# Twelve weight loads of a sparse-attention-and-FFN kernel, each issued as two transfers of 64 partitions

## The chip, the cores and the metric

The kernel runs on one core of a Trainium2 chip. The metric is device time in microseconds (us), measured from the start of the program's launch on the chip to its end; three runs of the kernel before gave 817.62, 818.4 and 819.12 us, median 818.4. Traces come from one profiled execution, with times counted from the start of its span.

## The reference

Attention with two sparse masks, then a feed-forward network with a gate. There are 8 batches, 8 heads, 576 positions and 64 elements per head; the network takes the 4608 tokens from 512 to 2048 and back to 512.

```
scores = matmul(q, k.T) / sqrt(64)
mask   = (0 <= rel < 32)                         for heads 0..3
         (rel >= 0) & (pos_k % 32 == pos_q % 32) for heads 4..7
attn   = softmax(where(mask, scores, -1e9))
x      = (attn @ v), heads side by side          # [4608, 512]
h      = x @ w_in                                # [4608, 2048]
g      = h if h >= 1; 0 if h <= -1; (h + 1)**2 / 4 between
out    = g @ w_out                               # [4608, 512]
```

## The kernel before, in words

The weights come in 8-byte numbers. The host part lays them out as `w[f, p, 1024]`: 16 units `f` of 128 columns of `w_in` (part `i = 0`, 512 numbers in each partition) and the 128 rows of `w_out` that belong to them (part `i = 1`). `load_w(f, i)` (L312 to L320) brings one part of one unit, 128 partitions of 4 KB, 512 KB in all, with one `dma_start` on SyncE's queue (SP, L319). Every part is then turned into two 4-byte tiles, a high and a low one, by five operations: A (ACT, L343), L (ACT, L347), B (DVE, L351), C (POOL, L355) on the raw words, then D (ACT or DVE, L364), which writes the high tile, and E (DVE, L368), which writes the low one. The matmuls of unit `f` (`up`, h, L775, and `down`, o, L820) read those tiles. `load_piece` (L322) loads the last two units in another way and isn't touched.

The first 3 chunks of 512 tokens go through `up`, the gate and `down` unit by unit; the other 3072 tokens go in three blocks through a form with seven products in place of eight (L917, L1005), whose factors are written to DRAM and fetched again. The attention of a batch is worked in four groups of scores: two of local heads (operands `qk_l`) and two of strided heads (`qk_s`); scores are L482, the turned probabilities go through PE's transposes, and for the later batches partly through DRAM (`spread`, L643, and `gather`, L654, which writes 32 partitions of the tile pT with each transfer).

All loads stand in one queue, SP, in the order of the code: at the start the four score operands of batch 0, then

```
load_w(0, 0, loaded[0, 1, "qk"][0:1, 0, 0:1])
load_v(0, 0); load_v(0, 1)
load_w(1, 0)
load_v(0, 2); load_v(0, 3)
load_w(2, 0)
stage(4)            # raw_0.1, raw_1.1, raw_2.1, raw_3.0, raw_3.1
for p in range(2): load_qk(1, p)
stage(6)            # raw_4.0, raw_4.1, raw_5.0, raw_5.1
```

(raw_3.1 stands for part 1 of unit 3, and so on; the lines are L1044 to L1055). The first load waits for an ACT copy (L318) that reads the score operands. The framework gives every transfer one of eight lanes in turn (DMAHW0 to DMAHW7 in the rows below), and an issue on a lane waits until the transfer before it on that lane, the eighth before, has landed. The order of the arithmetic is written out by hand in tables (BEGIN for the start, CONV for the conversions), so no scheduler moves it.

Of the kernel before, what the change touches and what calls it, by code (L numbers as in the profile page):

```python
# [17 lines left out]
P = 128  # L18
# [155 lines left out]
def tile_sparse_attention_then_ffn(  # L174
# [14 lines left out]
    nc = tc.nc  # L189
# [112 lines left out]
    wt, raws, pieces, held = {}, {}, {}, set()  # L302
    PLACES = (6, 7, 8, 9, 10, 11, 12, 13, 14, 15, 12, 13, 14, 15)
    w_v = w.bitcast(U32).rearrange("f p (i e t) -> f p i e t", i=2, t=2)
# [4 lines left out]
    def place(u, shape, dtype, name):  # L309
        return slot(f"w{u}", shape, dtype, name)  # L310

    def load_w(f, i, after=None):  # L312
        at = PLACES[f]
        if i == 0:
            held.add(at)
            raws[f] = place(at, [P, 2, DM, 2], U32, f"raw_{f}")
        if after is not None:
            nc.scalar.copy(raws[f][0:1, i, 0:1, 0].bitcast(F32), after)  # L318
        nc.sync.dma_start(raws[f][:, i], w_v[f][:, i])  # L319
        pieces[f, i] = [(raws[f][:, i], slice(0, DM))]  # L320

    def load_piece(f, i, k=0, pool=qk_p, tag="qk", of=1):  # L322
# [51 lines left out]
    def stage(n=len(PLACES)):  # L374
        nonlocal staged
        while staged < n and ((staged, 0) in pieces or PLACES[staged] not in held):
            if (staged, 0) not in pieces:
                load_w(staged, 0)
            load_w(staged, 1)
            staged += 1  # L380
# [662 lines left out]
    with tc.manual_schedule():  # L1043
        for p in range(4):  # L1044
            load_qk(0, p)
        load_w(0, 0, loaded[0, 1, "qk"][0:1, 0, 0:1])
        load_v(0, 0)
        load_v(0, 1)
# [127 lines left out]
```

## Time and profile before

| | |
|---|---|
| median of three runs | 818.4 us |
| the profiled execution: span | 815.5 us |
| the profiled execution: its own time beside the span | some 2.9 us around it, if it is a median run |
| PE busy | 806.2 us, 99% of the span |
| DVE, ACT, POOL busy | 574.7, 495.4, 232.5 us |
| bytes moved | 195.10 MB, mean 239 GB/s |
| granted TensorE clock | full in all 40 slices |

PE is TensorE, DVE VectorE, ACT ScalarE, POOL GpSimd, SP SyncE. PE is the engine that sets the time of most of the span; the DMA engines are at full share only in the first 40 us or so and at some places later. The profiled execution's own time wasn't recorded apart from the three runs; the 2.9 us are the median less the span.

### The profile page before, as it was taken

How to read it: one execution, taken by the hardware profiler on the slowest of the kernel's cores; microseconds unless marked ns; L12 is line 12 of the kernel's file. 1: busy time of each engine (PE TensorE's matmuls, PEld its weight loads, DVE VectorE, ACT ScalarE, POOL GpSimd, SP SyncE). 2: the span in 40 equal slices, each digit the busy share in tenths (PEclk: the TensorE clock that was granted, in tenths of full speed). 3: DMA queues.
4: the chain of work that ended last, by engine and by line, in shares of the span. 5: the costliest groups of instructions: out<-in, count | busy, mean ns of one | idle time of the engine just before them, and what ended most of it. 6: DMA issues, size and time to landing. Idle time of an engine off the chain costs nothing.

```text
span 815.5 us, 17861 instructions
## 1 busy us (share of the span) xinstructions
PE 806.2 (99%) x6969; PEld 656.9 (81%) x6969; DVE 574.7 (70%) x850; ACT 495.4 (61%) x866; POOL 232.5 (29%) x226
## 2 busy tenths in 40 slices
PE   8999999999999999999999999999999999999998
PEld 6788888878878888887878888888888888888886
DVE  5898868767548477776778876675589834558664
ACT  5888955545355365776775453778654647775442
POOL 5353544873347543023222000220120001114100
PEclk9999999999999999999999999999999999999999
DMA  9936437788868867987998768887666776666765
GB/s 344 408 138 201 153 111 274 265 298 278 265 221 299 286 243 257 304 287 247 285 288 266 216 203 249 263 265 228 193 193 213 232 235 196 196 192 190 216 200 170
DMA packets 101796, 195.10 MB, mean 239 GB/s; under 512 B 17105, under 2 KB 32465, under 8 KB 99665
## 3 DMA queue, kind: packets, MB, share of 16 engines
q1 hardware_dynamic: 92496, 164.60, 63.3%
q10 hardware_dynamic: 9216, 29.36, 9.4%
q8 instruction: 55, 0.90, 0.5%
q14 instruction: 29, 0.23, 0.1%
HBM read 147.26 MB, written 46.66 MB: 238 GB/s over the span
## 4 chain that ended last, share of the span: by engine, by line
PE 91%; DMA 5%; issue 1%; DVE 1%; ACT 1%; POOL 0%; SPq 0%; ACTq 0%; POOLq 0%
PE o L820 16%; PE h L775 16%; PE yo L1005 15%; PE y L917 15%; PE zo L1005 8%; PE z L917 7%; PE xo L1005 4%; PE x L917 4%; PE xp L669 3%; PE sc L482 3%; DMA wr<-kq 1%; DMA qk<-in_qk_s 1%; DMA there<-t 1%; DMA pT<-there 1%; DMA qk<-in_qk_l 1%
## 5 line engine op out<-in xcount | busy, mean ns | idle before, releaser
L917 PE MATMUL y<-x,wr 128*128 128x512 f32 x576 | 141.3, 392 | 0.0
L775 PE MATMUL h<-xq,w 128*128 128x512 f32 x576 | 140.0, 392 | 0.1
L1005 PE MATMUL yo<-hl,wr 128*128 128x512 f32 x576 | 132.8, 390 | 0.6 <-DMA wr<-kq 0.6
L820 PE MATMUL o<-gh,w 128*128 128x512 f32 x384 | 130.1, 399 | 0.0
L1005 PEld LDWEIGHTS yo<-hl,wr 128*128 128x128 f32 x576 | 108.0, 188 | 23.4 <-DMA wr<-kq 1.0
L775 PEld LDWEIGHTS h<-xq,w 128*128 128x128 f32 x576 | 107.4, 188 | 23.4 <-DVE xq L739 0.7
L917 PEld LDWEIGHTS y<-x,wr 128*128 128x128 f32 x576 | 107.4, 188 | 22.7
L820 PEld LDWEIGHTS o<-gh,w 128*128 128x128 f32 x384 | 72.1, 188 | 16.2
L820 PE MATMUL o<-gl,w 128*128 128x512 f32 x192 | 75.0, 391 | 0.0
L917 PE MATMUL z<-x,wr 128*128 128x512 f32 x288 | 73.7, 391 | 0.0
L957 POOL TENSOR_TENSOR ga<-gb,ga 128x1024 f32<-128x1024 f32 x9 | 21.6, 2397 | 167.5 <-DVE ga L785 141.7
L1005 PE MATMUL zo<-hl,wr 128*128 128x512 f32 x288 | 66.1, 390 | 0.0
L572 POOL TENSOR_TENSOR pr<-pr,st 128x384 f32<-128x384 f32 (+3 forms) x21 | 26.3, 1253 | 135.7 <-DVE st L595 64.5
L1005 PEld LDWEIGHTS zo<-hl,wr 128*128 128x128 f32 x288 | 54.0, 188 | 11.3
L917 PEld LDWEIGHTS z<-x,wr 128*128 128x128 f32 x288 | 53.8, 188 | 11.3
L782 ACT ACTIVATE tmp<-tmp 128x512 f32<-128x512 f32 x96 | 60.7, 632 | 3.0
L871 DVE TENSOR_TENSOR hl<-ga,hl 128x1024 fp32r<-128x1024 f32 x36 | 47.3, 1315 | 19.9 <-ACT hl L870 18.2
L870 ACT CAST hl<-ga 128x1024 fp32r<-128x1024 f32 x36 | 38.0, 1056 | 35.1 <-PE yo L1005 12.6
L396 POOL TENSOR_TENSOR xs<-w 128x512 f32<-128x512 f32 x32 | 45.1, 1426 | 48.4 <-DMA ks<-xs 32.8
L785 DVE SCALAR_TENSOR_TENSOR h<-h,u 128x512 f32<-128x512 f32 x47 | 32.8, 697 | 30.5 <-ACT u L782 30.1
L398 POOL TENSOR_TENSOR xs<-xs 128x256 f32<-128x256 f32 x64 | 51.3, 802 | 5.0
L779 ACT ACTIVATE u<-h,half 128x512 f32<-128x512 f32 x48 | 33.1, 689 | 29.6 <-PE h L775 24.1
(120 smaller groups left out, 1321.9 us busy)
## 6 DMA issues: line engine op xcount, KB each, us to landing
wr<-ks SPq DMA_DIRECT2D x192, 256.0 KB, 3.9
wr<-kq SPq DMA_DIRECT2D x144, 256.0 KB, 3.4
ks<-xs ACTq DMA_DIRECT2D x16, 1024.0 KB, 4.8
raw<-in_w SPq DMA_DIRECT2D x30, 512.0 KB, 9.6
kq<-w ACTq DMA_DIRECT2D x48, 256.0 KB, 3.8
qk<-in_qk_s SPq DMA_DIRECT2D x16, 604.0 KB, 6.1
qk<-in_qk_l SPq DMA_DIRECT2D x16, 576.0 KB, 6.0
v<-in_v_l SPq DMA_DIRECT2D x21, 384.0 KB, 6.0
```

Of the source, the lines that this page charges most:

```text
L396: nc.gpsimd.tensor_tensor(out=b[:, :, f] if i else b[:, f], in0=hi, in1=lo, op=ALU.add)
L398: nc.gpsimd.tensor_tensor(out=st[:, to, HF:], in0=st[:, x, HF:], in1=st[:, y, HF:], op=op)
L572: eng.tensor_tensor(out=pr, in0=pr, in1=st[:, 0].unsqueeze(2).broadcast_to(list(pr.shape)), op=ALU.add)
L775: nc.tensor.matmul(o_ps[c, f], wt[f][:, 0, h, x, e:e + P], xq[c][:, y, cc], start=first and n == 0, stop=last and n == len(todo) - 1)
L779: nc.scalar.activation(u, h, AF.Relu, bias=half, scale=0.5)
L782: nc.scalar.activation(u, u, AF.Square)
L785: nc.vector.scalar_tensor_tensor(out=to, in0=h, scalar=1.0, in1=u, op0=ALU.max, op1=ALU.min)
L820: nc.tensor.matmul(o_ps[c][d], wt[f][:, 1, h, x, e:e + P], gs[y], start=f == 0 and n == 0, stop=f == NF - 1 and n == 2)
L870: nc.scalar.copy(t[:, 0], src)
L871: nc.vector.tensor_tensor(out=t[:, 1], in0=src, in1=t[:, 0].bitcast(F32), op=ALU.subtract)
L917: nc.tensor.matmul(to, w_[:, a, c * P:(c + 1) * P], xc[m][:, b, c], start=m in (1, 2, 5) and c + q == 0, stop=c == 1 and q == 2, skip_grou ...
L1005: nc.tensor.matmul(to, w_[jj][:, a, d * P:(d + 1) * P], t[:, b, jj], start=m in (1, 2, 5) and k + jj + q == 0, stop=k == NP // 2 - 1 and j ...
```

## The change

For the units 0 to 5 one load becomes two, of partitions 0 to 63 and 64 to 127, 256 KB each; the other units load as before. Twelve calls of `load_w` are concerned, so twelve transfers more are issued.

```
-        nc.sync.dma_start(raws[f][:, i], w_v[f][:, i])
+        n = P // 2 if f < 6 else P
+        for p in range(0, P, n):
+            nc.sync.dma_start(raws[f][p:p + n, i], w_v[f][p:p + n, i])
```

The rows of SP's queue from the second raw_1 load on, before: each row is an issue, with the lane that it waits for in brackets.

```order
L319 DMA raw_1_198<-in_w 128x1024
L431 DMA v_0_2_None_200<-in_v_s 128x768 [waits DMAHW0_49]
L431 DMA v_0_3_202<-in_v_s 128x640 [waits DMAHW1_49]
L319 DMA raw_2_204<-in_w 128x1024 [waits DMAHW2_49]
L319 DMA raw_0_191<-in_w 128x1024 [waits DMAHW3_49]
L319 DMA raw_1_198<-in_w 128x1024 [waits DMAHW4_49]
```

The same place now:

```order
L321 DMA raw_1_199<-in_w 64x1024 [waits DMAHW0_49]
L321 DMA raw_1_199<-in_w 64x1024 [waits DMAHW1_49]
L433 DMA v_0_2_None_202<-in_v_s 128x768 [waits DMAHW2_49]
L433 DMA v_0_3_204<-in_v_s 128x640 [waits DMAHW3_49]
L321 DMA raw_2_206<-in_w 64x1024 [waits DMAHW4_49]
L321 DMA raw_2_206<-in_w 64x1024 [waits DMAHW5_49]
L321 DMA raw_0_191<-in_w 64x1024 [waits DMAHW6_49]
L321 DMA raw_0_191<-in_w 64x1024 [waits DMAHW7_49]
```

Every raw load up to unit 5 stands twice, and each half takes a lane of its own, so the eight transfers that may be out hold fewer bytes here. The queue has 634 rows where it had 622.

On ACT, the rows around the first conversion of raw_1, before:

```order
L343 ACTIVATE raw_1_198<-raw_1_198 128x512 [waits DMAHW7_49]
L364 CAST w_0_516<-raw_0_191 128x2x256 [waits Pool_49]
L587 ACTIVATE st_0_3_411<-st_0_3_411 128x10 [waits DVE_49]
L730 CAST xq_0_147<-xp_0_0_0_366 128x384 [waits PE_49]
L730 CAST xq_0_147<-xp_0_0_1_367 128x384 [waits PE_49]
L347 ACTIVATE raw_1_198<-raw_1_198 128x512
L343 ACTIVATE raw_2_204<-raw_2_204 128x512 [waits DMAHW2_49]
```

And now:

```order
L345 ACTIVATE raw_1_199<-raw_1_199 128x512 [waits DMAHW1_49,DMAHW0_49]
L366 CAST w_0_528<-raw_0_191 128x2x256 [waits Pool_49]
L589 ACTIVATE st_0_3_423<-st_0_3_423 128x10 [waits DVE_49]
L732 CAST xq_0_147<-xp_0_0_0_378 128x384 [waits PE_49]
L732 CAST xq_0_147<-xp_0_0_1_379 128x384 [waits PE_49]
L349 ACTIVATE raw_1_199<-raw_1_199 128x512
L345 ACTIVATE raw_2_206<-raw_2_206 128x512 [waits DMAHW5_49,DMAHW4_49]
```

The order of ACT's rows is the same; a conversion that waited for one lane now waits for two. The other engines' rows keep their order and number as well. Lines behind L319 stand two further on.

## Rows read from the trace of the kernel before

**Rows 1.** The page: span, busy times, granted clock, and the chain of waits by engine.
```profile
span 815.5 us, 17861 instructions
...
PE 806.2 (99%) x6969; PEld 656.9 (81%) x6969; DVE 574.7 (70%) x850; ACT 495.4 (61%) x866; POOL 232.5 (29%) x226
...
PEclk9999999999999999999999999999999999999999
...
PE 91%; DMA 5%; issue 1%; DVE 1%; ACT 1%; POOL 0%; SPq 0%; ACTq 0%; POOLq 0%
```
**Rows 2.** Windows: stretch, length, busy PE, PEld, DVE, ACT, POOL, clock, DMA share, GB/s.
```profile
10.00:20.00 10.00, 8.51 (x220) 6.85 (x221) 9.17 (x20) 8.31 (x22) 6.14 (x7) 1.00 1.00 389
20.00:27.00 7.00, 5.91 (x108) 4.28 (x105) 6.39 (x19) 5.03 (x20) 2.27 (x3) 1.00 1.04 415
27.00:40.00 13.00, 12.92 (x171) 10.29 (x176) 11.28 (x27) 12.48 (x23) 5.12 (x5) 1.00 1.02 404
...
50.00:60.00 10.00, 10.00 (x92) 8.15 (x91) 9.86 (x20) 8.59 (x16) 5.02 (x6) 1.00 0.01 2
```
**Rows 3.** Waits of SP's queue, 0 to 60 us: total, times, longest, in us.
```profile
SPq L319 <- DMA raw<-in_w: 9.5, 9, 2.1
```
**Rows 4.** Timeline of SP: start, us, then the issue; narrow stretches and 0 to 60 us.
```profile
6.61 0.33 SPq L319 DMA_DIRECT2D raw<-in_w  x1
...
7.93 0.69 SPq L319 DMA_DIRECT2D raw<-in_w  x1
...
10.25 0.64 SPq L319 DMA_DIRECT2D raw<-in_w  x1
...
18.61 0.33 SPq L418 DMA_DIRECT2D qk<-in_qk_l  x1
```
**Rows 5.** DMA view of those four issues: count, KB, us from issue to landing.
```profile
raw<-in_w SPq DMA_DIRECT2D x1, 512.0 KB, 4.8
...
raw<-in_w SPq DMA_DIRECT2D x1, 512.0 KB, 8.8
...
raw<-in_w SPq DMA_DIRECT2D x1, 512.0 KB, 9.6
...
qk<-in_qk_l SPq DMA_DIRECT2D x1, 576.0 KB, 10.5
```
**Rows 6.** DMA view, 30 to 36 us, raw loads of 128 partitions in a row.
```profile
DMA packets 730, 2.42 MB, mean 403 GB/s; under 512 B 81, under 2 KB 81, under 8 KB 727
```
**Rows 7.** Timeline of PE, 20 to 36 us: start, us, instruction, count.
```profile
24.06 6.28 PE L775 MATMUL h<-xq,w 128*128 128x512 f32 x24
30.27 1.17 PE L482 MATMUL sc<-qk 64*32 64x64 f32 x96
31.37 3.04 PE L775 MATMUL h<-xq,w 128*128 128x512 f32 x12
```
**Rows 8.** Timeline of ACT, 10.9 to 24.2 us, with idle time before and its releaser.
```profile
11.42 0.68 ACT L343 ACTIVATE raw<-raw 128x512 f32<-128x512 f32 x1 [0.93 <-DMA raw<-in_w]
...
16.97 0.71 ACT L343 ACTIVATE raw<-raw 128x512 f32<-128x512 f32 x1
...
19.93 0.70 ACT L343 ACTIVATE raw<-raw 128x512 f32<-128x512 f32 x1
```
**Rows 9.** DMA view of gathers into 32 partitions: 171.2:171.6, 521.6:522.3, 522.3:523.0, 521.6:523.0.
```profile
DMA packets 195, 0.14 MB, mean 361 GB/s; under 512 B 22, under 2 KB 191, under 8 KB 194
...
DMA packets 313, 0.23 MB, mean 334 GB/s; under 512 B 36, under 2 KB 297, under 8 KB 313
...
DMA packets 181, 0.14 MB, mean 205 GB/s; under 512 B 22, under 2 KB 164, under 8 KB 181
...
DMA packets 494, 0.38 MB, mean 270 GB/s; under 512 B 58, under 2 KB 461, under 8 KB 494
```
**Rows 10.** Timeline of SP, 519 to 524 us: the issue of the gathers.
```profile
519.26 1.81 SPq L654 DMA_DIRECT2D pT<-there  x4
```

## The prediction

> **What bounds the kernel now.** The page comes first. PE is busy 99% of the span, its granted clock is full in every slice, and the chain of waits is 91% PE; DMA holds 5% of it [rows 1]. So time can be lost or won only where PE is not yet, or no longer, the end of the chain. The windows say where that is: PE is busy 8.51 of 10 us from 10 to 20 us and 5.91 of 7 up to 27 us, but 12.92 of 13 from 27 to 40 us and all of the stretch after 50 us [rows 2]. From 27 us on there is next to nothing that could absorb a delay: what PE starts later there, it ends later. The last column but one of the same rows is the share of the DMA engines: 1.00 to 1.04 until 40 us, 0.01 after 50 us. In the first 40 us, then, the 16 DMA engines have no free time either, and the transfers stand behind one another in the order in which SP issued them. The changed loads lie in just this stretch.
>
> The queue's waits confirm that SP is ahead of the engines: it waited nine times, 9.5 us in all, because a raw load eight transfers back hadn't landed [rows 3]. An issue and its landing are 4.8 us apart for the first raw load, 9.6 and 10.5 us for later ones [rows 4, 5], while one load of 512 KB takes 512 KB / 403 GB/s = 1.30 us of the engines' time [rows 6]. The rest is queueing.
>
> **What each part of the change costs.** *Twelve more issues on SP.* An issue takes 0.33 to 0.69 us [rows 4], a half load 0.65 us of the engines. Issuing stays at least level with draining, and behind eight outstanding halves lie 8 x 0.65 = 5.2 us of transfers, so the engines don't run dry; cost 0. If SP fell behind by the difference (0.69 less 0.65, 24 times) it would be 1 us, and the stock of 5.2 us covers it.
>
> *Half the bytes under the eight lanes.* Issues come later, landings don't, for as long as the engines have a stock; cost 0. A gain isn't excluded by this term alone, but I find none: the first half of a load lands earlier, and every reader waits for both halves.
>
> *Two waits on a reader in place of one.* The later half decides, and at an equal rate it lands when the whole load landed; cost 0.
>
> *The rate of a transfer that fills only 64 partitions.* Every transfer of this stretch so far fills 128, so the trace has no such row. The nearest are the gathers into 32 partitions, four in a row, two into each half of the tile [rows 10]. At the start of one such burst the engines move 361 GB/s, in another 334 GB/s, and in the 0.7 us after that only 205 GB/s, at full share both times; that burst as a whole makes 270 GB/s [rows 9]. Against the 403 GB/s of the 128-partition loads [rows 6] a transfer would be longer by a factor of 403/361 = 1.12 at one end, 403/205 = 1.97 at the other, and 403/270 = 1.49 over a burst. Packets of the gathers are smaller than those of the raw loads, which excuses some of this; that is why 1.0 is kept as the lower bound. I take 1.49, since the changed loads too come as bursts that change the half of the tile with each transfer, and a burst's mean holds both its quick beginning and its slow remainder.
>
> [...]
>
> *What such a factor does.* With a factor r one load costs e = (r - 1) x 1.30 us more, and since the engines work without a gap, each later landing is late by e for every split load ahead of it. I follow that to three readers.
>
> ACT converts raw_1 at 16.97 us; its load lands at 7.93 + 8.8 = 16.7 us, two split loads in, so it is late if 2e is over 0.2. Raw_2 lands at 10.25 + 9.6 = 19.85 us and is converted at 19.93 us [rows 4, 5, 8], with 3e and 0.1 us to spare. The first of all, raw_0, ends an idle of ACT as it is, at 11.42 us [rows 8]. So ACT, and through it the first matmuls of h, are late by up to 3e - 0.1.
>
> PE's scores of batch 1 decide more. They start at 30.27 us and take 1.17 us; the second half of them reads the second operand qk_l, needed at 30.27 + 0.58 = 30.85 us [rows 7]. That operand was issued at 18.61 us and lands 10.5 us later, at 29.1 us [rows 4, 5], behind eight split loads: parts 0 of units 0, 1 and 2, parts 1 of the same, and both of unit 3. So it is late by 8e - 1.7 us, and PE behind it has 12.92 of 13 us filled [rows 2]. The two delays lie on one clock and aren't added; PE waits for the later, which is this one as soon as 5e is over 1.6.
>
> At r = 1.49: e = 0.64 us, 8e = 5.1, less 1.7 = **3.4 us**. Four more loads are split after this (units 4 and 5), 4e = 2.6 us; what they delay is needed by a PE that is itself 3.4 us later, so nothing is added.
>
> The sum: 0 + 0 + 0 + 3.4. It is made against the profiled execution, 815.5 us of span and, by the median, some 2.9 us around it; on the median of 818.4 us it gives **821.8 us**.
>
> **The rivals.** *B, the halves run as fast as the whole, and it is not slower.* At 361 GB/s e is 0.16 us and 8e = 1.2 is under the 1.7 us of slack; what is left is ACT's 3e - 0.1 = 0.4 at most, of which part is lost in the idle PE has before 27 us. Up to r = 1.32 (8e = 1.7 + 1.64) the end moves by less than 0.2%, or 1.64 us, which is about what a measurement of this kernel can tell from no change. For it: two of the three short gather stretches are near the full rate, and as the 16 engines aren't in step some can be in the next half, in other partitions, while the others are still in this one. Against it: the 205 GB/s at full share. The time: 818.4 to 819, taken as 818.4.
>
> *C, strictly half the rate.* r = 1.97, e = 1.26, 8e = 10.1, less 1.7 = 8.4: 826.8 us. For it: the 205 GB/s last as long as the window is wide. Against it: the same burst began at 334. PE would then stand still for several us before 31 us; the granted clock is 1.00 in every stretch [rows 2], so no row here shows what a fallen clock costs. If the 12 matmuls of 3.04 us [rows 7] ran at half the clock, that would be 3.0 us more.
>
> *D, faster.* Something would have to land earlier and be waited for. The only waits of ACT on raw loads are the 0.93 us before raw_0 [rows 8], and its later half comes no earlier than the whole did, unless two shorter transfers pass the engines quicker than one. Bound: 0.9 us, not seen anywhere.
>
> That the change doesn't do what it says is excluded by the order of SP's queue, where the halves stand.
>
> **How the numbers follow.** The forecast (r from 1.32 to 1.85, 820 to 825.5 us) gets 0.44, as the burst's mean is the nearest row. B gets 0.30: everything else costs 0 and r below 1.32 is enough. C gets 0.22, D 0.04. So faster 0.04, same 0.30, slower 0.44 + 0.22 = 0.66. The range starts below B's time by half its spread of runs, 817.8, since B holds more than the 0.2 that may be left out, and ends at 827.6, which takes in C without a fallen clock; outside are D, part of B's spread, and C with its clock fallen.
>
> **What would show it.** Right: the DMA windows from 7 to 25 us show full share at about 270 GB/s instead of 389 to 415; the second qk_l of batch 1 lands 5 us later than 29.1; PE's scores have an idle behind that transfer of 2 us or more, and the matmuls of h behind them start some 3.4 us later, with no change in their durations; after 60 us nothing differs. ACT's L345 on raw_1 and raw_2 shows idle released by a raw load. Wrong: GB/s near 400 through the stretch and a landing of that operand near 29 us (B), landings 10 us late or a granted clock below 1.00 (C), or halves that are issued so late that the DMA share falls below 1, which would put the cost on SP's issues instead.

## The result and the profile after

The change is slower: 827.67 us median of five runs (826.56 to 831.26) against 817.62 us of the kernel before in the same comparison, a ratio of 1.0136 (95% interval 1.0115 to 1.0157). Forecast was 821.8 us in a range up to 827.6. The execution that was profiled is the longest of its five, 831.26 us, 3.6 us over their median.

The page of the change: span, busy times, and the chain of waits by engine.

```profile
span 829.5 us, 17896 instructions
...
PE 812.6 (98%) x6969; PEld 661.2 (80%) x6969; DVE 574.7 (69%) x850; ACT 496.7 (60%) x866; POOL 231.7 (28%) x226
...
PE 90%; DMA 8%; SPq 1%; issue 1%; ACT 0%; DVE 0%; ACTq 0%
```

DMA's part of the chain has risen from 5% [rows 1] to 8%. Where this lies, the windows of the change tell (stretch, length, busy PE, PEld, DVE, ACT, POOL, granted clock, DMA share, GB/s):

```profile
10.00:20.00 10.00, 7.56 (x197) 5.89 (x190) 8.05 (x16) 5.68 (x16) 4.92 (x6) 1.00 1.02 276
20.00:27.00 7.00, 3.07 (x79) 2.55 (x75) 3.93 (x10) 4.38 (x14) 2.35 (x3) 0.93 1.04 233
27.00:40.00 13.00, 10.28 (x146) 8.27 (x139) 9.01 (x27) 9.33 (x25) 2.73 (x3) 0.76 1.03 246
40.00:50.00 10.00, 9.36 (x75) 7.49 (x76) 6.35 (x12) 6.70 (x13) 3.47 (x5) 0.68 1.03 286
50.00:60.00 10.00, 10.00 (x90) 8.03 (x89) 9.83 (x19) 8.87 (x16) 6.28 (x5) 1.00 1.03 409
```

The DMA share is as full as before, but it moves 233 and 246 GB/s where it moved 415 and 404 [rows 2]. That is a busy engine that gets less done, not one that lacks issues. PE is busy 3.07 of 7 us where it was busy 5.91, and behind that its granted clock, 1.00 throughout before [rows 1], is 0.76 and 0.68 on the mean, and 0.50 from 27 to 32 us and from 40 to 46 us. Once the last split load is through, from 50 us on, the rate is 409 GB/s again.

The two readers that the prediction followed, on ACT (timeline, with the idle before and what ended it) and on PE:

```profile
12.61 0.67 ACT L345 ACTIVATE raw<-raw 128x512 f32<-128x512 f32 x1 [2.53 <-DMA raw<-in_w]
...
19.43 0.68 ACT L345 ACTIVATE raw<-raw 128x512 f32<-128x512 f32 x1 [1.27 <-DMA raw<-in_w]
...
24.70 0.67 ACT L345 ACTIVATE raw<-raw 128x512 f32<-128x512 f32 x1 [2.62 <-DMA raw<-in_w]
```

```profile
28.93 7.52 PE L777 MATMUL h<-xq,w 128*128 128x512 f32 x24
37.84 0.82 PE L484 MATMUL sc<-qk 64*32 64x64 f32 x48 [1.39 <-DMA qk<-in_qk_l]
40.64 0.97 PE L484 MATMUL sc<-qk 64*32 64x64 f32 x48 [1.98 <-DMA qk<-in_qk_l]
41.54 5.30 PE L777 MATMUL h<-xq,w 128*128 128x512 f32 x12
```

Raw_2 is converted at 24.70 us in place of 19.93 [rows 8], 4.8 us later, and the first matmuls of h start 4.9 us later than 24.06 [rows 7]. The second half of batch 1's scores starts at 40.64 us where it was due at 30.85, 9.8 us later, at the landing of the second qk_l. That operand was issued at 28.98 us and took 11.6:

```profile
28.98 0.33 SPq L420 DMA_DIRECT2D qk<-in_qk_l  x1
```

```profile
qk<-in_qk_l SPq DMA_DIRECT2D x1, 576.0 KB, 11.6
```

So it landed at 40.6 us instead of 29.1 [rows 4, 5], 11.5 us late. Eight split loads stand ahead of it in the queue and four behind it. Put down to the eight alone this would be 1.43 us for each, and the expectations below reckon with that; the experiments show that the four behind have a part in it too. Of the profile's 14.0 us of longer span, 9.8 lie here; 2.3 more in the 12 matmuls of h behind it, which take 5.30 us in place of 3.04 [rows 7], at a granted clock of 0.53 over them. A row of PE behind the whole stretch, 48 scores of strided heads, shows the sum of it, before and now:

```profile
57.94 0.92 PE L482 MATMUL sc<-qk 64*64 64x54 f32 x48
...
70.22 0.92 PE L484 MATMUL sc<-qk 64*64 64x54 f32 x48
```

This row is 12.3 us late; the other 1.7 us of the span come after it. What comes after it differs in every profile of this case, from 1.3 us less to 2.6 us more than before, so this row compares the versions better than their spans do.

### The profile page after: what moved, and what is told of

Its sections match the earlier page's. It is cut to its first block, busy times and chain, and to the rows that moved or that the text cites. A ratio compares the mean times of both kernels' runs of the same rounds, so it can differ in the third digit from the quotient of the medians.

```text
span 829.5 us, 17896 instructions
## 1 busy us (share of the span) xinstructions
PE 812.6 (98%) x6969; PEld 661.2 (80%) x6969; DVE 574.7 (69%) x850; ACT 496.7 (60%) x866; POOL 231.7 (28%) x226
## 4 chain that ended last, share of the span: by engine, by line
PE 90%; DMA 8%; SPq 1%; issue 1%; ACT 0%; DVE 0%; ACTq 0%
PE o L822 16%; PE yo L1007 16%; PE h L777 15%; PE y L919 14%; PE zo L1007 8%; PE z L919 7%; PE xo L1007 4%; PE xp L671 4%; PE x L919 3%; PE sc L484 3%; DMA raw<-in_w 2%; DMA qk<-in_qk_l 2%; DMA pT<-there 1%; DMA there<-t 1%; DMA wr<-kq 1%; DMA wr<-ks 1%
## 5 line engine op out<-in xcount | busy, mean ns | idle before, releaser
L777 PE MATMUL h<-xq,w 128*128 128x512 f32 x576 | 143.3, 399 | 0.0
L777 PEld LDWEIGHTS h<-xq,w 128*128 128x128 f32 x576 | 110.5, 193 | 23.7 <-issue 0.2
```

The costliest lines, as they stand in the source:

```text
L777: nc.tensor.matmul(o_ps[c, f], wt[f][:, 0, h, x, e:e + P], xq[c][:, y, cc], start=first and n == 0, stop=last and n == len(todo) - 1)
```

## The experiments

The theory (P): which partitions a transfer fills decides its rate, and the contiguous halves, 0 to 63 and 64 to 127, are the slow ones. Rivals: any transfer of 64 partitions is slow (N); twice the transfers with half the bytes behind eight lanes are slow (Q). Times are medians of the runs; a ratio is to the kernel before on the same chip, and a loss in us given beside a ratio is worked out from it.

### Rates of loads by themselves

Two kernels of loads alone, in stretches; the first:

```
whole():   for u in 32 parts: load(u)                                    # 128 partitions
halves():  for u in 16 parts: load(u, 0:64);  load(u, 64:128)
low():     for u in 32 parts: load(u, 0:64)
columns(): for u in 16 parts: load(u, first 2 KB); load(u, last 2 KB)    # 128 partitions
middle():  for u in 32 parts: load(u, 32:96)
turned():  as halves, the second of every two parts with 64:128 first
```

> A kernel of loads alone: it leaves out the whole computation and writes zeros, so only its trace counts. Stretches one after the other, each of 8 MB with the loads back to back on SP's queue: whole loads of 128 partitions (512 KB, 16 MB of them); halves 0-63 and 64-127 in turn (256 KB each); only the halves 0-63; two transfers of 128 partitions and 2 KB each; only partitions 32-95; halves in turned order (low, high, high, low). [...] Rival Q (twice the transfers and half the bytes behind the eight lanes are slow): halves, low halves, columns and 32-95 all about 1.07 us.

Windows inside those six stretches, in that order (stretch, length, busy DVE, busy POOL, clock, DMA share, GB/s). The fourth and fifth are short pieces, from the quickest part of their stretches:

```profile
15.00:40.00 25.00, 3.32 (x19) 0.00 (x0) 1.00 1.03 410
50.00:80.00 30.00, 2.45 (x14) 0.00 (x0) 1.00 1.04 234
90.00:125.00 35.00, 4.90 (x28) 0.00 (x0) 1.00 1.04 210
149.00:153.00 4.00, 0.52 (x3) 0.00 (x0) 1.00 1.05 401
176.00:180.00 4.00, 1.05 (x6) 0.00 (x0) 1.00 1.01 406
187.00:220.00 33.00, 2.58 (x15) 0.00 (x0) 1.00 1.04 224
```

Longer pieces of the fourth and the fifth, with slower spells in them, show less:

```profile
137.00:146.00 9.00, 1.05 (x6) 0.00 (x0) 1.00 1.00 357
163.00:180.00 17.00, 4.06 (x24) 0.00 (x0) 1.00 1.01 377
```

Halves in turn run at 234 GB/s, a factor of 410/234 = 1.75; halves on one side only at 210, a factor of 1.95. Columns, twice the transfers of the same bytes, run at 357 to 401, far above 234, so Q falls as the cause, though it may cost a little. Partitions 32 to 95 are 64 partitions too and run at 377 to 406, so N falls. (The rows read in DRAM shift along with the partitions, so these runs don't tell which end of the transfer it is that decides.) In turned order, where two halves of the same side follow one another, the rate is 4% lower than in plain turn. The engines then are at full share in every one of these stretches and move half as much in some.

The second:

```
strided(): for u in 16 parts: load(u, 0::2); load(u, 1::2)               # even, odd partitions
queues():  as halves, 0:64 on SP's queue and 64:128 on ACT's
mixed():   whole load of one part, then the two halves of the next, and so on
halves()
```

> A kernel of loads alone again, without the computation. Stretches: whole loads; even and odd partitions (256 KB each); halves 0-63 on SP's queue and 64-127 on ACT's queue; whole loads in turn with pairs of halves; halves in turn. Theory P: even and odd 0.65 us each; the two queues no quicker than one, 1.07 to 1.3 us a half; in the mixed stretch 512 KB whole plus 512 KB in halves take 1.28 + 2.24 = 3.5 us if a whole load keeps its price, and up to 4.0 us if whole loads behind halves are slowed as well, which the landings of v and qk_l in the change suggest (1.9 and 2.9 us in place of 1.4). Rival: two queues fill both halves of SBUF at once, 0.65 us a half.

```profile
54.00:62.00 8.00, 1.05 (x6) 0.00 (x0) 1.00 1.02 397
78.00:108.00 30.00, 2.27 (x13) 0.00 (x0) 1.00 1.04 236
118.00:144.00 26.00, 2.10 (x12) 0.00 (x0) 1.00 1.03 243
155.00:185.00 30.00, 2.27 (x13) 0.00 (x0) 1.00 1.04 233
```

Even and odd partitions run at 397 GB/s. Two queues give 236, no more than one. The mixed stretch is the surprise. If whole loads kept 410 and halves 234 GB/s, equal bytes of both would run at 2/(1/410 + 1/234) = 298. They run at 243, so 1 MB takes 4.3 us instead of 3.5. Mixing the two kinds costs 0.8 us for each pair of loads beyond what the halves cost by themselves; these windows don't tell how it is shared.

### Columns, and even and odd partitions, in the kernel

```
-        n = P // 2 if f < 6 else P
-        for p in range(0, P, n):
-            nc.sync.dma_start(raws[f][p:p + n, i], w_v[f][p:p + n, i])
+        n = DM // 2 if f < 6 else DM
+        for e in range(0, DM, n):
+            nc.sync.dma_start(raws[f][:, i, e:e + n], w_v[f][:, i, e:e + n])
```

> The loads of the six units in two transfers again, but cut by columns: 128 partitions of 2 KB each, so the same number of transfers, the same bytes of each, the same waits on lanes. Theories P and N: about the time of the kernel before, 817.6 us, within 2 us, the second qk_l of batch 1 landing near 29 us. Rival Q: about 827.7 us, the operand landing near 40 us.

818.8 us; ratio to the kernel before 1.0014 (0.9995 to 1.0033). The same twelve additional transfers, lanes and waits cost nothing that the interval separates from zero. (In its profile the loads run at 346 GB/s from 20 to 27 us, under the 415 of before, so a little may be lost; by the interval's end it is 2.7 us at most.)

```
-        n = P // 2 if f < 6 else P
-        for p in range(0, P, n):
-            nc.sync.dma_start(raws[f][p:p + n, i], w_v[f][p:p + n, i])
+        n = 2 if f < 6 else 1
+        for p in range(n):
+            nc.sync.dma_start(raws[f][p:P:n, i], w_v[f][p:P:n, i])
```

> The loads of the six units in two transfers of 64 partitions again, but the even partitions and the odd ones, which are spread over the whole height. Theory P: nearer to the kernel before than to the change, 818 to 821 us. Rival N: about 827.7 us. Rival Q: about 827.7 us.

818.75 us; 1.0017 (0.9997 to 1.0037). Transfers of 64 partitions each, as in the change, but spread, and the loss is gone, or 3.0 us at most by the interval's end. P stands in the kernel too.

### Which loads cost

Each time the change's condition is narrowed. The last four loads alone:

```
-        n = P // 2 if f < 6 else P
+        n = P // 2 if 4 <= f < 6 else P
```

> Halves 0-63 and 64-127 as in the change, but only for units 4 and 5: the four loads that come behind the second qk_l of batch 1. If the loss comes by that operand, as the trace says: 817.6 to 819.5 us, since the four land up to 4 x 1.4 = 5.7 us later and their readers have some slack. If it comes from the loads' number wherever they are: a third of the 10 us, 821 us.

818.72 us; 1.0017 (1.0002 to 1.0032), 1.4 us, or 0.2 to 2.6 by the interval. Its windows show the slow stretch without an effect on PE:

```profile
27.00:40.00 13.00, 12.92 (x146) 10.25 (x146) 11.20 (x28) 12.07 (x22) 4.66 (x5) 1.00 1.02 229
```

229 GB/s here, and PE is busy 12.92 of 13 us as before [rows 2]. But the two operands qk_l of batch 1, which have no split load ahead of them here, tell of a cost all the same (the issue of each, and its time to landing):

```profile
17.27 0.33 SPq L420 DMA_DIRECT2D qk<-in_qk_l  x1
qk<-in_qk_l SPq DMA_DIRECT2D x1, 576.0 KB, 10.5
...
18.06 0.33 SPq L420 DMA_DIRECT2D qk<-in_qk_l  x1
qk<-in_qk_l SPq DMA_DIRECT2D x1, 576.0 KB, 12.8
```

They land at 27.8 and 30.9 us, 3.1 us apart, where before it was 1.5 (27.66 and 29.14 us). A whole transfer is late here by halves that stand behind it in the queue. PE doesn't show it because the prediction's slack of 1.7 us just covers it.

The eight loads ahead of the operand:

```
-        n = P // 2 if f < 6 else P
+        n = P // 2 if f < 4 else P
```

> Halves as in the change, but only for units 0 to 3: the eight loads ahead of the second qk_l of batch 1. If that operand's landing sets the loss: 826 to 828.5 us, the whole of it. If the loss goes by the number of split loads: two thirds, 824.4 us.

826.25 us; 1.0096 (1.0061 to 1.0131). This interval holds the lower end of the change's, so whether the last four add something when the others are split is not told apart by the times; the two thirds by number, 824.4 us (1.0083), lie in it as well. The trace says more. Its two operands, with whole loads behind them:

```profile
29.16 0.33 SPq L420 DMA_DIRECT2D qk<-in_qk_l  x1
qk<-in_qk_l SPq DMA_DIRECT2D x1, 576.0 KB, 8.7
...
30.23 0.33 SPq L420 DMA_DIRECT2D qk<-in_qk_l  x1
qk<-in_qk_l SPq DMA_DIRECT2D x1, 576.0 KB, 9.0
```

They land at 37.9 and 39.2 us, 1.4 us apart, nearly as before, where the change has 37.7 and 40.6, 2.9 us apart. So the last four, behind the operand, add some 1.5 us to its lateness in the change. PE's row of strided scores is 8.3 us late here instead of 12.3 (one profile each), and the 12 matmuls of h keep their duration:

```profile
39.92 3.02 PE L777 MATMUL h<-xq,w 128*128 128x512 f32 x12
...
66.26 0.92 PE L484 MATMUL sc<-qk 64*64 64x54 f32 x48
```

The first three:

```
-        n = P // 2 if f < 6 else P
+        n = P // 2 if f < 3 and i == 0 else P
```

> Halves only for the first three loads, parts 0 of units 0, 1 and 2. They are ahead of the conversions of raw_1 and raw_2 on ACT and so of the first matmuls of h, and ahead of the second qk_l of batch 1 too. By landings 1.43 us late for each: raw_2 some 4.3 us late, the first matmuls of h from 24.1 to about 28 us, and behind them 4 us of loss, 821 to 822.5 us; the operand lands at 33.4 us, no later than PE gets to it. If only the operand counts: 3 x 1.43 - 1.7 = 2.6 us, 820 us.

822.54 us; 1.0059 (1.0041 to 1.0076), or 4.8 us. PE and the operand:

```profile
28.53 6.32 PE L777 MATMUL h<-xq,w 128*128 128x512 f32 x24
34.78 1.17 PE L484 MATMUL sc<-qk 64*32 64x64 f32 x96
```

The 24 matmuls of h start 4.5 us later than before and run at their old 6.3 us; the scores behind them wait for no transfer. This is the conversions' way alone.

The next five:

```
-        n = P // 2 if f < 6 else P
+        n = P // 2 if f < 4 and (i == 1 or f == 3) else P
```

> Halves only for the five loads behind those: parts 1 of units 0, 1 and 2, and both parts of unit 3. ACT's conversions of raw_1 and raw_2 and the first matmuls of h stay where they were; the operand lands 5 x 1.43 = 7.2 us late and PE waits 5.4 us for it: 822 to 823.5 us, and a lower granted clock behind the wait. If the loss comes by the conversions alone: 818 us.

820.91 us; 1.0052 (1.0037 to 1.0068), or 4.3 us, a little under what was expected, and by another way:

```profile
27.13 7.44 PE L777 MATMUL h<-xq,w 128*128 128x512 f32 x24
34.50 1.35 PE L484 MATMUL sc<-qk 64*32 64x64 f32 x96
```

The matmuls of h don't stay where they were: they start 3.1 us late and take 7.44 us, 1.2 us more, with a granted clock of 0.85 from 27 to 40 us, and so reach the scores 4.2 us late, at about the time when the operand lands; no idle by a transfer stands ahead of the scores. The three loads ahead of them weren't split, yet ACT waits for raw_2, which it had at 19.93 us before [rows 8], and the stretch from 20 to 27 us has a granted clock of 0.78:

```profile
20.96 0.68 ACT L345 ACTIVATE raw<-raw 128x512 f32<-128x512 f32 x1 [0.74 <-DMA raw<-in_w]
```

```profile
20.00:27.00 7.00, 3.72 (x98) 3.08 (x96) 4.17 (x13) 3.62 (x13) 2.44 (x3) 0.78 1.04 245
```

So a whole load with halves behind it in the queue is 1.0 us late, as the second operand was with the last four loads split: the mixing cost of the second kernel of loads, seen in this one. What makes 3.1 us at PE of this 1.0 us isn't shown.

The two parts, 4.8 and 4.3 us, add up to 9.1, within the interval for all eight (5.0 to 10.7 us). This doesn't say that ACT's way and the operand's add up: the five loads cost by raw_2 and the clock, not by the operand.

### Order of the loads

```
         load_w(2, 0)
+        for p in range(2):
+            load_qk(1, p)
         stage(4)
-        for p in range(2):
-            load_qk(1, p)
```

> The change with the two qk_l of batch 1 issued ahead of raw_0.1, raw_1.1, raw_2.1, raw_3.0 and raw_3.1 instead of behind them, so with three split loads before them, not eight. If their landing sets the end: they land some 12 us earlier, PE no longer waits for them, and the time falls to 819 to 823 us, held by the raw parts that now land about 4 us later. Rival: the bytes decide, in whatever order, since all of them are needed soon: 826 to 828 us.

824.67 us; 1.0091 (1.0065 to 1.0117), more than the 819 to 823 us expected. The scores no longer wait, and the raw parts take their place as the end of the chain, which up to 60 us now reads, by line:

```profile
by line: DMA raw<-in_w 63.7%; DMA qk<-in_qk_l 8.0%; PE h L777 4.3%; ACT raw L349 2.1%; DVE w L370 2.1%; issue 2.1%; SPq L321 1.9%; SPq L433 1.7%; ACT raw L345 1.6%; DVE pr L544 1.5%; ACT pr L581 1.4%; DVE gh L807 1.2%; DVE h L787 1.2%; PE t
```

Its interval just meets the change's. In its profile PE's row of strided scores starts at 65.40 us, 7.5 us late instead of 12.3. So the order counts, and the rival, that the bytes are needed in whatever order, is half right: the time lies between the two forecasts.

### The fallen clock

```
-e2 w0 Zf0:5 f0 p1 x3 c0 B00 v0 b3 L00 e3 r1 q2 p2 f1 C00 r2 q3 A10 d1 D00 p3 h0 r3 L10 l0 A20 v1 B10
+e2 w0 Zf0:5 f0 p1 x3 c0 B00 v0 b3 L00 e3 r1 q2 p2 f1 C00 r2 q3 A10 d1 D00 p3 h0 r3 L10 l0 A20 Zv1:14 v1 B10
...
-WORK = {1: [(-60.38, 's0'),
+WORK = {1: [(-60.38, 'Zs0:14 s0'),
```

(`Zv1:14` is 14 matmuls of zeros into the bank that step v1 then fills.)

> The change with 28 matmuls of zeros more on PE (14 ahead of the value step of batch 0's second group, 14 ahead of batch 1's first scores), put where PE stood idle, so that the clock is not let fall; what they write is overwritten. If the fallen clock behind the scores costs what the rows show (12 matmuls in 5.30 us in place of 3.04): 2.3 us less, about 825.4 us, and a granted clock of 1.00 from 40 to 50 us. Rival: the fall lies wholly beside waits for transfers; 827.7 us as before, or more by what the zeros delay.

The profile does what was asked: the 12 matmuls behind the scores are back at 3.01 us, and the granted clock is 1.00 from 40 to 50 us, where the change has 0.68.

```profile
41.40 0.72 PE L484 MATMUL sc<-qk 64*32 64x64 f32 x48 [1.74 <-DMA qk<-in_qk_l]
42.05 3.01 PE L777 MATMUL h<-xq,w 128*128 128x512 f32 x12
```

The time doesn't: 828.88 us, 1.014 (1.0109 to 1.0172). So the change was run once more beside a version with only the second 14 zeros.

> The change itself once more, unaltered, for a second profile and more runs on the chip of the next kernel. If the profile of the change is typical: granted clock about 0.7 from 40 to 50 us, the 12 matmuls of h behind batch 1's scores in 5.3 us, and about 1.4% over the kernel before. If the fallen clock there is an accident of that one execution: 3.0 us for the 12, and a span some 2 to 4 us under the 829.5 us seen.

826.28 us; 1.0099 (1.0074 to 1.0123), 8.1 us and under the 1.4% expected. The second profile of the change repeats the first, with a granted clock of 0.69 from 40 to 50 us:

```profile
40.65 0.97 PE L484 MATMUL sc<-qk 64*32 64x64 f32 x48 [1.91 <-DMA qk<-in_qk_l]
41.55 5.17 PE L777 MATMUL h<-xq,w 128*128 128x512 f32 x12
```

The profiled execution, 830.2 us, is again the longest of its set.

> The change with 14 matmuls of zeros ahead of batch 1's first scores alone (the 14 ahead of the value step are left out, since they may have delayed what came behind them). If the clock is a part of the loss: granted clock 1.00 from 40 to 50 us and 1 to 2.3 us less than the change run beside it. If it isn't: the same time within 1 us, and the loss is the transfers' alone.

831.07 us; 1.0158 (1.0132 to 1.0183): 0.6% over the change beside it, though its 12 matmuls take 3.03 us, at a granted clock of 1.00 from 40 to 50 us. In its profile the 24 matmuls of h before the scores start at 30.38 us, later than the change's 28.93, but that isn't the zeros' doing: raw_0 is already 1.3 us later than the change's 12.61 us, 23 us ahead of them.

```profile
13.87 0.66 ACT L345 ACTIVATE raw<-raw 128x512 f32<-128x512 f32 x1 [3.67 <-DMA raw<-in_w]
```

PE's row of strided scores comes earlier with zeros than without: the change again, then 28 zeros, then 14:

```profile
70.06 0.92 PE L484 MATMUL sc<-qk 64*64 64x54 f32 x48
...
68.39 0.92 PE L484 MATMUL sc<-qk 64*64 64x54 f32 x48
...
68.82 0.92 PE L484 MATMUL sc<-qk 64*64 64x54 f32 x48
```

That is 12.1, 10.5 and 10.9 us late, so up to this row the zeros gave back 1.2 to 1.8 us in the profiles. Behind it the last one loses 2.6 us more. Where, and why its runs are slower, wasn't found, so the price of the clock in the change stays open between 0 and the 2.3 us that the rows show.

## Why the prediction was wrong

**The bound, and where the change acts: right.** 12.3 of the profile's 14.0 us are lost up to the row of strided scores, all of it at full DMA share, and the two readers named are those that are late [rows 2, 7, 8]. That nothing would differ after 60 us isn't borne out by the profile: 1.7 us come behind that row, of which no run shows the cause.

**Issues, lanes, two waits: right.** They were put at 0. Columns have all three and measure 1.0014 (0.9995 to 1.0033).

**The rate of the halves: the first step that failed, a term mis-sized.** I took a factor of 1.49 from the mean of a burst of gathers [rows 9], e = 0.64 us for a load. Halves in turn by themselves run at 234 GB/s, a factor of 1.75 against 410, e = 0.75 x 1.28 = 0.96 us; this alone makes 8e - 1.7 = 6.0 us in place of the 3.4. The 205 GB/s were the nearer row: halves on one side alone have 210. The quick start of a burst, which I let weigh as much, isn't there in a long row of halves. Nor was the 270 a mean of the whole burst: its four gathers, issued from 519.26 us on [rows 10], land from 523.1 us on, behind the end of its window.

```profile
pT<-there SPq DMA_DIRECT2D x4, 96.0 KB, 3.8
```

That smaller packets excuse some of the gathers' rate (theirs are 0.7 to 0.8 KB on the mean) fits the trace before: packets of some 0.6 KB from 128 partitions to DRAM ran at 279 GB/s at full share there (180.1 to 180.6 us), those of 4 KB loads at 403 [rows 6]; how much of it they excuse isn't shown. Rival B's reason, that some engines can be in the next half meanwhile, bought little: packets of two transfers in a row are under way together in the trace before (4.8 KB ones of a score operand and 4 KB ones of raw_0 from 8.0 to 8.8 us), but the halves in turn, at 234 GB/s, are only a tenth above the 210 of one side alone. Why that is so, and why partitions 32 to 95 have 406, no run shows.

**What mixing costs: put at nothing, the second step that failed and the larger.** I gave whole transfers among the halves their old price, and let a landing be late only by split loads ahead of it. The mixed stretch shows 243 GB/s where 298 would be due. From the landing of raw_0 to that of the operand 7 split loads, 1856 KB of v and 1152 KB of qk_l pass, 6.75 MB; at 243 GB/s that is 27.8 us, and the trace of the change has 28.1 (12.5 to 40.6), where before there were 17.7. Of the operand's 11.5 us, 8 x 0.96 = 7.7 are then the halves' own, and the other 3.8 come with the whole transfers among them, some 1.5 of these by the four split loads behind the operand. The last four and the next five loads, split alone, both show a whole transfer late by halves behind it. How it comes about stays open.

**The operand's lateness, 8e - 1.7: the right reader and the right slack, a form that lacks the loads behind.** The scores were 9.8 us late. (With e = 1.43 the form gives 9.7, but that e is the lateness itself, divided by eight.) By the medians of five runs the kernel lost 10.05 us, in the second comparison 8.8. Rival C named nearly this size, 8.4 us, and its signs came, a landing 10 us late and a granted clock below 1.00. But it had the size from a factor of 1.97, where the halves in turn show 1.75 and mixing makes up the rest; that is in part luck.

**ACT's way: undersized.** 3e - 0.1 with e = 0.64 made 1.8 us; it was 4.8, and where no operand is late it is the loss: the first three loads alone cost 4.8 us. That the two ways lie beside one another was right in the change: PE reaches the scores at 28.93 + 7.52 = 36.45 us, 6.2 late, and the operand's 9.8 hold that.

**The last four loads at 0: wrong in the change.** I looked only at what they delay behind them. Split alone they cost 1.4 us (0.2 to 2.6), as the slack takes up the operand's delay; behind the other eight they add some 1.5 us to it.

**The clock: an end of rival C that came about in the profile**, 5.30 in place of 3.04 us; its share in the runs' time isn't settled. I kept it out of the range, which the result missed by 0.1 us. That the miss is so small is luck, as the range ended at C's time, not at one worked out from the rate and the mixing. (Its lower end, half the spread of 1.5 us below 818.4, is 817.65 and not 817.8; nothing hangs on it.)

## What to carry to other kernels

A load that fills SBUF in contiguous halves took 1.75 times its time here although the engines show full share; read GB/s beside the share. If a load must be cut, cut it along the columns or into partitions that are spread over the height: both kept all or most of the rate here by themselves (357 to 401 and 397 of 410 GB/s), and the kernel lost 3.0 us at most. Before calling a delay hidden, price what a slow transfer does to the whole transfers around it in the queue, those ahead of it too, and look which reader comes first. And a part that costs next to nothing when tried alone may only have been covered by slack that the other parts use up.

## What was not expected

Whole loads and halves in turn run at 243 GB/s where their own rates give 298, and a whole load can be late by halves that were issued behind it (1.6 us for the second operand with the last four loads split alone); why was not followed up. Two queues, one for each half, run no quicker than one (236 and 234 GB/s). And matmuls of zeros that kept the granted clock at 1.00 in the place where it had fallen made the kernel no faster by its runs, though PE was 1.2 to 1.8 us less late behind that place in the profiles.
